# Logit slots of whole keys in two parts instead of three, with a new order

## The chip, the core and the metric

The kernel runs on one core of a Trainium2 chip. The metric is the device time of one execution in microseconds. A core has five engines that work side by side and wait for each other by semaphores: TensorE (PE, with its weight loads as PEld), VectorE (DVE), ScalarE (ACT), GpSimd (POOL) and SyncE (SP, which here only issues transfers).

## What is computed

The input `x` has 2048 tokens of 512. One branch is attention with a compressive memory: 32 heads of 16, four segments of 512 tokens, causal softmax within a segment, and a memory `M`, `z` of all earlier segments. The other is a gated MLP with 1792 hidden columns. A gate per token mixes both.

```python
phi = lambda t: jnp.where(t > 0, t + 1.0, jnp.exp(t))
for s in range(N):
    logits = jnp.einsum('bhqd,bhkd->bhqk', qs, ks) * scale + mask
    p = _softmax(logits, axis=-1)
    a_dot = jnp.einsum('bhqk,bhkd->bhqd', p, vs)
    num = jnp.einsum('bhld,bhde->bhle', phi(qs), M)
    den = jnp.einsum('bhld,bhd->bhl', phi(qs), z)[..., None] + 1e-06
    outs.append(g * num / den + (1.0 - g) * a_dot)
    M = M + jnp.einsum('bhld,bhle->bhde', phi(ks), vs)
    z = z + jnp.einsum('bhld->bhd', phi(ks))
...
h = _gelu(x @ w_gate) * (x @ w_up)
return gate * (o @ wo) + (1 - gate) * (h @ w_down)
```

## The kernel before

**Tasks and their order.** The kernel is a list of some 1340 tasks. The string ORDER (L35 on) names them one by one, and `Sched.run` issues them in that order; each engine works through its own tasks in it and waits where data or a buffer is not ready. A word is a name, then `#` with the letters of the buffers that it takes (in the order of its allocations), and `@A`, `@D`, `@P` or `@S` where a task may run on several engines: ACT, DVE, POOL or SP. The numbers in a name are mostly segment and part: `up2.8` is the product with columns 8 x 128 of `w_up` for segment 2.

**TensorE's tasks.** `q`, `k`, `v`, `gt` and `up` are products of a segment with weights (`gt` two column blocks at once), `dn` and `wo` accumulate one output tile of 128 tokens: 14 `dn` steps and then four `wo` steps, which read the attention output that `o` has written into `xT`. Nearly all run as four matmuls side by side on tiles of 32 columns of the array (`mm4`, L389); I call such four a batch. `den`, `num` and `M` belong to the memory. The last segment's last output tile is split in 384 (`h0`) and 128 columns (`h1`).

**Slots.** Causal logits of a segment are computed in 18 logit slots, nine for each pair of chunks of eight heads. A slot is a PSUM tile of two halves of [128, 2, 512]: `lg` writes it (L695; four heads side by side on tiles of 32 rows, one bank each), `ex...a` and `ex...b` take the exponential of each half on ACT into a `pT` buffer (L231), and `as...a`, `as...b` set what lies above the diagonal to zero on POOL. Keys come in four tiles of 128. For each, the 64 queries beside the first half of the keys are put into a slot of their own (`e == 2`, mask at L722); the rest, 448, 320, 192 and 64 queries for the four key tiles, fills two whole-key slots (`e` 0 for even heads, 1 for odd ones), by the table FULL: each entry is key tile, offset, columns, and place in the slot. Only the first 64 columns of a key tile lie on the diagonal. With three parts a slot, tile 0 was split so that both masked stretches of the slot begin 256 columns apart, and one POOL operation of four stretches of 64 masks a half (L727):

```python
FULL = (((0, 0, 256, 0), (3, 0, 64, 256), (0, 256, 192, 320)),
        ((1, 0, 256, 0), (2, 0, 192, 256), (1, 256, 64, 448)))
```

**From slot to output.** `pv` (L756) multiplies the parts of its slots with the values, for the even (`e`) or odd (`o`) heads of a chunk: six whole-key parts and four of 64 queries, in the order PVO. On DVE, `epv` transposes the result (L773), `r`, `rg` and `n` divide by the sum and weigh (L783, L786, L791), `m` adds the memory part (L796, DVE or POOL), and `o` transposes into `xT` (L799). `pv3.3o` is the last of the 32 groups, and `o3.3` the last `o`. `os` scales an output tile, `st` stores it.

**Buffers.** Slots, `gt` and `num` share three pairs of PSUM banks (`lg`, letters a to c); the other products have two banks (`gen`). `pT` has eleven buffers. `wos` scales a part of `wo` once, `ke` and `ko` make key copies for odd heads, `vh` makes value copies, `ek`, `eq` and `ev` take products out of PSUM.

Of the kernel before, what the change touches and what calls it, by code (L numbers as in the profile page):

```python
# [9 lines left out]
ALU = mybir.AluOpType  # L10
# [3 lines left out]
P = 128  # L14
D = 512
# [13 lines left out]
HB = P // 2  # L29
# [7 lines left out]
k0f1.0 xt0.1 xt1.1 xt2.1 ext0.1 xt3.1 ext1.1 k0f2.0 ext2.1 ext3.1 k0f3.0 k0f0.1 k0f1.1 k0f2.1  # L37
k0f3.1 q0.0#ba ek0.1@A ek0.3@D ek0.2@D q0.1#a eq0.0@D ke0.2@A#a gt0.0#b eq0.1@A ke0.3@D ek0.0@D
Ek0.1#a ke0.0@D#b ke0.1@D ko0.1@A lg0#ac Emk0.1 v0.2#b Qk0.1@D#a ex0a#a v0.1#a ev0.2@D ex0b#b as0a
ko0.3@D gt0.1#a ko0.0@D as0b ev0.1@D ko0.2@P egt0.0#a gt0.6#c phk0.1@P#a egt0.1#b gt0.3#b egt0.6#c  # L40
gt1.6#a egt0.3#d pk0.1#a v0.0#b egt1.6#e v0.3#a ev0.0@D lg1#cb ev0.3@D q0.2#bb ex1b#c vh0.1@D
q0.3#a eq0.2@D ex1a#d lg2#ab eq0.3@D k1.0#bc ex2b#e as1a lx2 as1b q1.0#ac ex2a#f lg3#cb z1.3
gt0.5#a ex3a#g z1.0 eq1.0@D Ek0.0#a z0.2 v1.0#a ex3b#h Qk0.0@D#a z3.3 gt1.0#c tb z0.0 omg#a
gt0.4#b egt0.5#f lx3 Emk0.0 ev1.0@D z3.2 k1.1#a egt0.4#g z3.0 gt0.2#a z2.1 ek1.0@A z2.2 egt1.0#h
ek1.1@D up0.0#b egt0.2#i z1.2 z1.1 lg4#bc up0.10#a z0.3 gt1.3#a z3.1 ex4b#i z2.3 wo vh0.0@D ex4a#j
gt1.4#c z2.0 z0.1 as4a eup0.10 as2a gt1.1#b egt1.3#j eup0.0 egt1.4#k M0.1#a q1.1#b egt1.1#l eM0.1
as2b up1.0#a eq1.1@D lg5#ac eup1.0 up0.11#b ex5a#k phk0.0@D#a as3b pv0.0e#aa eup0.11 pk0.0#b
Eq1.0#a zsp2 lg6#ba epv0.0e up0.7#b ex6b#a zsp0 up0.6#a eup0.7 ex6a#b as4b up1.3#b as6b eup0.6
ex5b#c as3a Emq1.0 as6a lg7#ab eup1.3 pv0.0o#a as5a ex7a#d as5b up0.3#b epv0.0o ex7b#g as7a lg8#ca
zsp1 eup0.3 pv0.1e#ab ex8b#h Qq1.0@D#a up0.5#b epv0.1e ex8a#i as8b lg9#ba as7b eup0.5 up0.4#a  # L50
ex9b#j as8a zsp3 pv0.1o#b eup0.4 ex9a#a lg10#ca ke1.0@D#b phq1.0@P#a up1.2#a epv0.1o g2 ex10b#b
r0.0#a up1.7#b eup1.2 ex10a#c r0.1#b lg11#ba rg0.0 up1.8#a n0.0#a Ek1.0#a as10a eup1.7 gt2.2#c
wos1@D ex11b#k Emk1.0 eb ex11a#d Qk1.0@D#a gt1.2#a phk1.0@D#a eup1.8 as11a pk1.0#a omz gt1.5#b
egt1.2#m egt2.2#n as9a gt2.4#a ke1.1@D egt1.5#o as11b M0.0#b egt2.4#p up0.1#a eM0.0 v1.3#b as9b
eup0.1 as10b lg12#cb ev1.3@D k1.2#aa ex12b#e rg0.1 ko1.1@D zbd0 q1.2#ba ex12a#f ek1.2@D as12b
wos2@P mbd0 lg13#ab eq1.2@A q1.3#a wdn3 ex13b#g pv0.2e#ba as12a eq1.3@D ex13a#h as13b lg14#cb
epv0.2e v1.1#a ex14a#i as13a up0.8#b ev1.1@D ex14b#a lg15#ac eup0.8 up1.13#a ex15b#b as14b as14a
pv0.2o#b ex15a#c eup1.13 lg16#bc epv0.2o up0.12#a ex16b#j n0.1#b up1.9#b ex16a#e r0.2#a as16b
eup0.12 as15b lg17#ac as15a eup1.9 v1.2#a ex17b#f ko1.0@D wos3@D pv0.3e#bb ex17a#g ev1.2@D as17b
lg18#bc as16a epv0.3e up0.13#a ex18a#h as17a ke1.2@D#a ko1.2@D k1.3#b Eq1.1#a eup0.13 wdn0 wos0@D  # L60
# [12 lines left out]
dn0.0.6 dn0.0.7 o0.3 dn0.0.8 ex31b#g up2.6#b Eq2.0#a lg32#bc eup2.6 dn0.0.9 dn0.0.10 as28b
dn0.0.11 ex31a#h dn0.0.12 as30b dn0.0.13 wo0.0.0 as31b pv1.2e#ba ex32a#i as31a wo0.0.1 as30a
wo0.0.2 epv1.2e wo0.0.3 ex32b#a lg33#ab os0.0@D#a up2.5#b ex33a#b ke2.0@D#b st0.0 r1.1#b pv1.2o#a
eup2.5 ex33b#c lg34#ca epv1.2o k2.2#bc ex34a#j ko2.0@D as33b dn0.3.0#a dn0.3.1 ek2.2@D as32b
dn0.3.2 ex34b#e as32a lg35#bc rg1.1 as33a Emq2.0 dn0.3.3 dn0.3.4 ex35a#f dn0.3.5 as34b n1.1#a
M1.1#b dn0.3.6 dn0.3.7 ke2.1@A eM1.1 lg36#ab ke2.2@D#a Qq2.0@D#a dn0.3.8 ex36b#g dn0.3.9
phq2.0@D#c dn0.3.10 dn0.3.11 dn0.3.12 ex36a#h dn0.3.13 pv1.3e#bb wo0.3.0 ex35b#a epv1.3e lg37#ba
as36a wo0.3.1 as35a wo0.3.2 as34a wo0.3.3 ex37b#b k2.3#b rma1.2 os0.3@D#b ex37a#c num1#ca v2.1#a  # L80
enum1.1#b rma1.3 ko2.1@A ek2.3@D gt2.5#b Ek2.0#a as35b enum1.0#a ev2.1@A as37a rmr1 pv1.3o#b
gt3.1#c rmg1 Emk2.0 epv1.3o egt2.5#t nm1.0@D#a ko2.2@A up1.10#a Qk2.0@D#a m1.0@P egt3.1#u
enum1.2#a up2.7#b eup1.10 nm1.1@P#b lg38#bc r1.3#a v2.2#a eup2.7 ex38a#i enum1.3#b dn0.2.0#b
dn0.2.1 dn0.2.2 rg1.3 phk2.0@D#a dn0.2.3 ev2.2@A lg39#ab ex38b#a nm1.2@D#c dn0.2.4 pk2.0#a dn0.2.5
dn0.1.0#a r1.2#b dn0.1.1 dn0.1.2 ke2.3@D ex39b#d zbd1 dn0.1.3 vh2.1@D dn0.1.4 dn0.2.6 rg1.2
dn0.2.7 ex39a#e o1.0 as39b lg40#cb dn0.2.8 as38a dn0.2.9 Ek2.1#a dn0.2.10 dn0.2.11 dn0.2.12
dn0.2.13 wo0.2.0 ex40a#f wo0.2.1 wo0.2.2 dn0.1.5 dn0.1.6 Qk2.1@A#a as38b dn0.1.7 dn0.1.8 dn0.1.9
gt3.5#a vh2.0@A ex40b#j as39a gt3.0#c as36b m1.1@P wo0.2.3 as40a egt3.5#a gt2.0#b os0.2@D#c as37b
as40b n1.3#b egt3.0#b st0.2 o1.1 dn0.1.10 dn0.1.11 egt2.0#i dn0.1.12 pv2.0e#bb dn0.1.13 wo0.1.0
epv2.0e wo0.1.1 wo0.1.2 wo0.1.3 Emk2.1 lg41#ac os0.1@D#a up2.9#b ex41b#k mbd1 st0.1 n1.2#a k3.2#aa  # L90
ex41a#b st0.3 eup2.9 m1.2@P lg42#bc ek3.2@D pv2.0o#b ex42a#c phk2.1@P#a up3.10#a epv2.0o ex42b#g
lg43#ab eup3.10 up2.11#b ex43b#h as41b pk2.1#b M2.0#a ex43a#d as41a lg44#cb eM2.0 as43b eup2.11
up2.0#a as42a ex44a#e as42b q2.3#b nm1.3@P#a eup2.0 ex44b#f r2.0#a lg45#ac as43a eq2.3@D pv2.1e#aa
ex45b#j as44b m1.3@D up2.13#b as44a epv2.1e Eq2.1#a lg46#bc eup2.13 q3.0#aa ex46b#b Emq2.1 ko2.3@D
q3.1#b Qq2.1@D#a eq3.0@A o1.3 phq2.1@P#a ex46a#c pv2.1o#a gt3.2#c epv2.1o ex45a#g eq3.1@A as46b
Eq3.0#a den2#aa lg47#ba eden2 up2.10#b ex47a#k Qq3.0@D#a Emq3.0 up2.3#a phq3.0@D#b ex47b#a as47a
gt3.3#b eup2.10 o1.2 rg2.0 gt3.4#a egt3.3#d as45a eup2.3 as45b egt3.2#g as47b M2.1#b v3.3#a
egt3.4#f eM2.1 k3.0#bb ev3.3@D as46a lg48#bc ek3.0@D rma2.0#a v3.2#a ex48a#d dn1.0.0#b dn1.0.1
ev3.2@D ex48b#e rma2.2 dn1.0.2 lg49#ab r2.1#b k3.1#a rg2.1 ex49a#f ke3.0@D#b n2.1#b dn1.0.3
dn1.0.4 ek3.1@D ex49b#h as49a lg50#ca as48a dn1.0.5 dn1.0.6 as48b ex50a#i pv2.2e#aa as49b dn1.0.7  # L100
rma2.3 dn1.0.8 epv2.2e ex50b#b dn1.0.9 dn1.0.10 lg51#bc up3.7#a ex51a#c rma2.1 dn1.0.11 ex51b#g
dn1.0.12 eup3.7 lg52#ab as50b dn1.0.13 rmr2 wo1.0.0 ex52a#j pv2.2o#a as51b wo1.0.1 wo1.0.2 epv2.2o
ex52b#d as52a wo1.0.3 num2#ca as50a v3.1#a as51a os1.0@A#c enum2.1#b r2.2#b ko3.1@A q3.2#bb
enum2.0#a ev3.1@A lg53#bc eq3.2@D q3.3#a ex53a#e rg2.2 n2.0#a up3.8#b eq3.3@A ke3.1@D rmg2 ex53b#f
nm2.0@P#b pv2.3e#ab eup3.8 gt3.6#b epv2.3e as52b as53a enum2.3#a as53b nm2.1@P#c pv2.3o#b egt3.6#c
up2.1#a epv2.3o m2.1@P lg54#cb eup2.1 up3.13#b ko3.0@P enum2.2#b ex54a#h up3.3#a eup3.13 ex54b#b
r2.3#a lg55#ac eup3.3 k3.3#b ex55b#c as54b up3.11#a as54a ek3.3@D ex55a#g as55b lg56#bc eup3.11
v3.0#b ex56b#i as55a o2.1 up3.0#a m2.0@D ev3.0@A n2.2#b ex56a#a lg57#ac zbd2 eup3.0 up3.6#b
# [88 lines left out]
def kernel(  # L197
# [15 lines left out]
    nc = tc.nc  # L213
# [39 lines left out]
    S = Sched(RINGS)  # L253
# [419 lines left out]
    def logit_slot(s, t):  # L673
# [25 lines left out]
        for i in cs:  # L699
            c = 2 * pr + i  # L700
# [423 lines left out]
```

## Time and profile before

| | us |
|---|---|
| median of 3 runs (266.87 to 267.15) | 267.0 |
| the profiled execution | 266.52 |
| its span, first to last instruction | 264.6 |
| pT, 144 exponentials on ACT, L231 | 137.9 busy |
| L722, 32 masks of the 64-query slots on POOL | 37.5 busy |
| L617, 56 products with G on DVE | 38.3 busy |

Rows of groups give the line, engine and operation, then output and inputs with their shapes, the count, after the bar the time in which at least one ran, the mean of one in ns, and after the second bar the idle time of the engine just before. Rows of a timeline or of the chain of waits begin with the start and the length in us and merge neighbours of one kind. Rows of windows give busy time and, in brackets, the count by engine. Rows of waits give the total in us, how often, and the longest. Matmuls overlap, so the length of one is more than the distance to the next.

### The profile page before, as it was taken

How to read it: one execution, taken by the hardware profiler on the slowest of the kernel's cores; microseconds unless marked ns; L12 is line 12 of the kernel's file. 1: busy time of each engine (PE TensorE's matmuls, PEld its weight loads, DVE VectorE, ACT ScalarE, POOL GpSimd, SP SyncE). 2: the span in 40 equal slices, each digit the busy share in tenths (PEclk: the TensorE clock that was granted, in tenths of full speed). 3: DMA queues.
4: the chain of work that ended last, by engine and by line, in shares of the span. 5: the costliest groups of instructions: out<-in, count | busy, mean ns of one | idle time of the engine just before them, and what ended most of it. 6: DMA issues, size and time to landing. Idle time of an engine off the chain costs nothing.

```text
span 264.6 us, 13767 instructions
## 1 busy us (share of the span) xinstructions
PE 260.2 (98%) x6300; PEld 140.7 (53%) x6300; DVE 176.5 (67%) x360; ACT 218.8 (83%) x255; POOL 148.6 (56%) x266
## 2 busy tenths in 40 slices
PE   8999999999999999999999999999999999999995
PEld 7644575555555555455554455555444555555553
DVE  1634895889479688767695277765878684576461
ACT  2598989999999999999999999999999989840002
POOL 8360106886633762785454746698486768829100
PEclk9999999999999999999999999999999999999999
DMA  7999974300500005200005012000000000001002
GB/s 232 349 210 319 206 85 102 43 7 19 145 5 2 2 5 132 72 5 22 6 2 42 21 46 43 2 5 2 5 4 2 2 5 22 22 26 63 22 22 82
DMA packets 23706, 15.96 MB, mean 60 GB/s; under 512 B 14048, under 2 KB 22624, under 8 KB 23648
## 3 DMA queue, kind: packets, MB, share of 16 engines
q1 hardware_dynamic: 22640, 14.30, 23.8%
q8 instruction: 49, 0.80, 1.3%
q10 hardware_dynamic: 1008, 0.79, 0.9%
q14 instruction: 9, 0.07, 0.1%
HBM read 9.84 MB, written 2.10 MB: 45 GB/s over the span
## 4 chain that ended last, share of the span: by engine, by line
PE 97%; ACT 1%; DVE 1%; issue 0%
PE dn L389 24%; PE up L389 19%; PE gt L389 18%; PE lg L695 9%; PE pv L756 7%; PE v L389 6%; PE q L389 5%; PE k L389 4%; PE k L385 2%; PE warm L385 1%; ACT pT L231 1%; PE q L385 1%; PE gt L385 1%; PE M L874 1%; PE xt L491 0%; PE num L965 0%
## 5 line engine op out<-in xcount | busy, mean ns | idle before, releaser
L231 ACT ACTIVATE pT<-lg 128x1024 bf16<-128x1024 f32 x144 | 137.9, 1026 | 5.8 <-PE lg L695 4.9
L727 POOL TENSOR_SCALAR_AFFINE_SELECT pT<-pT 128x256 bf16<-128x256 bf16 x128 | 53.1, 439 | 63.2 <-ACT pT L231 59.0
L389 PE MATMUL dn<-wdn,G 128*32 128x512 bf16 (+2 forms) x952 | 58.1, 367 | 0.0
L389 PE MATMUL up<-xT,wup 128*32 128x512 bf16 x896 | 57.1, 380 | 0.0
L389 PE MATMUL gt<-xT,wga 128*32 128x512 bf16 x864 | 49.4, 379 | 0.0
L617 DVE TENSOR_TENSOR G<-up,G 128x512 bf16<-128x512 f32 x56 | 38.3, 684 | 14.2 <-PE up L389 13.2
L722 POOL TENSOR_SCALAR_AFFINE_SELECT pT<-pT 64x1024 bf16<-64x1024 bf16 x32 | 37.5, 1173 | 9.6 <-ACT pT L231 8.5
L389 PEld LDWEIGHTS <-wga 128*32 128x32 bf16 x864 | 24.5, 97 | 21.1 <-issue 0.2
L389 PEld LDWEIGHTS <-G 128*32 128x32 bf16 x952 | 22.7, 96 | 20.4 <-issue 0.2
L389 PEld LDWEIGHTS <-wup 128*32 128x32 bf16 x896 | 22.0, 96 | 18.8 <-issue 0.2
L773 DVE STREAM_TRANSPOSE T<-pv 128x512 f32<-128x512 f32 x32 | 22.9, 714 | 12.8 <-PE pv L756 12.6
L231 ACT ACTIVATE G<-gt 128x1024 bf16<-128x1024 f32 x28 | 27.7, 1018 | 3.7 <-PE gt L389 3.5
L1027 ACT ACTIVATE osb<-dn,omz 128x512 bf16<-128x512 f32 (+1 forms) x4 | 2.5, 614 | 25.3 <-PE dn L389 25.3
L229 ACT ACT_TABLE_LOAD x18 | 23.1, 1283 | 0.3
L1029 DVE TENSOR_SCALAR osb<-dn,omz 128x512 bf16<-128x512 f32 (+1 forms) x13 | 9.6, 740 | 17.8 <-PE dn L389 17.8
L756 PE MATMUL pv<-pT,vz 128*32 128x256 bf16 (+2 forms) x768 | 20.8, 238 | 0.0
L756 PEld LDWEIGHTS <-vz 128*32 128x32 bf16 x768 | 16.3, 97 | 6.6 <-ACT qT L235 0.7
L389 PE MATMUL dn<-wo,xT 128*32 128x512 bf16 (+2 forms) x272 | 19.2, 367 | 0.0
L389 PEld LDWEIGHTS <-xT 128*32 128x32 bf16 x528 | 12.8, 96 | 11.2 <-issue 0.5
L695 PEld LDWEIGHTS <-kO 32*128 32x128 bf16 x640 | 9.7, 92 | 15.1 <-issue 14.2
L934 POOL TENSOR_SCALAR rm<-Tm 32x32 f32<-32x32 f32 x48 | 14.1, 294 | 5.1 <-DVE Tm L928 2.0
L695 PE MATMUL lg<-qT,kO 32*128 32x64 bf16 (+2 forms) x640 | 16.4, 217 | 0.1
(112 smaller groups left out, 330.2 us busy)
## 6 DMA issues: line engine op xcount, KB each, us to landing
wup<-in_B_w_up_dram SPq DMA_DIRECT2D x1, 1792.0 KB, 9.8
out_dram<-osb SPq DMA_DIRECT2D x14, 128.0 KB, 1.7
wdn<-in_B_w_down_dram SPq DMA_DIRECT2D x3, 512.0 KB, 5.3
wga<-in_B_w_gate_dram SPq DMA_DIRECT2D x1, 1280.0 KB, 9.6
wdn<-in_A_x_dram SPq DMA_DIRECT2D x2, 512.0 KB, 10.2
wq<-in_A_wq_dram SPq DMA_DIRECT2D x1, 512.0 KB, 5.5
wga<-in_B_w_gate_dram SPq DMA_DIRECT2D x1, 512.0 KB, 6.4
wv<-in_A_wv_dram SPq DMA_DIRECT2D x1, 512.0 KB, 6.7
```

The lines of the kernel that those rows point to most:

```text
L229: nc.scalar.activation(nil[0][:, 1:2], nil[0][:, 0:1], func)
L231: nc.scalar.activation(dst, src, func, **kw)
L385: nc.tensor.matmul(out, lhsT=lhsT, rhs=rhs, start=start, stop=stop)
L389: nc.tensor.matmul(out[a], lhsT=lhsT[:, a], rhs=rhs, start=start, stop=stop, tile_position=(0, 32 * j), skip_group_check=True)
L617: UPT[(s, hs)] = evac("DVE", g, box, lambda e, t: nc.vector.tensor_mul(G[(s, hs // 2)][:, hs % 2, :], t[:, :], G[(s, hs // 2)][:, hs % 2, ...
L695: nc.tensor.matmul(A[j // 2][:, j % 2, at:at + n], lhsT=l, rhs=q[a, i, q0:q0 + n], start=True, stop=True, tile_position=(32 * j, 0))
L722: nc.gpsimd.affine_select(out=v, in_=v, pattern=[[0, 16], [1, HB]], compare_op=ALU.is_ge, fill=0.0, base=0, channel_multiplier=-1)
L727: nc.gpsimd.affine_select(out=v, in_=v, pattern=[[0, 4], [1, HB]], compare_op=ALU.is_ge, fill=0.0, base=HB, channel_multiplier=-1)
L756: nc.tensor.matmul(t[m:m + 32, q0:q0 + n], lhsT=v, rhs=pT[(s, u, j // 2)][:, j % 2, at:at + n], start=(n_ == 0), stop=(n_ == len(parts) - ...
L773: nc.vector.transpose(TT[key][:, e, :, :].rearrange("p a b -> p (a b)"), t[:, :])
L934: eng_of[e].tensor_scalar_add(RMt[s][32 * ((j + c) % 4):32 * ((j + c) % 4) + 32, c, :, :], bx["Td"][32 * c:32 * c + 32, :, 2 * j:2 * j + 2 ...
L1029: nc.vector.tensor_scalar_mul(bx["o"][:, lo:hi], box["t"][:, 0:hi - lo], g)
```

## The change

FULL has two parts a slot: 448 and 64 columns, or 320 and 192. `lg` issues 8 matmuls for a whole-key slot where it issued 12, `pv` 32 where it issued 40. The masked stretches of a slot no longer lie at equal distance, so `fa` issues two POOL operations per half, each of two stretches of 64. `Sched`, the slots, the buffers and all other tasks are the same; ORDER is another order of the same 1342 words, with other buffer letters and engines for some.

```diff
-    PVO = (0, 1, 2, 5, 3, 6, 4, 7, 8, 9)
-    FULL = (((0, 0, 256, 0), (3, 0, 64, 256), (0, 256, 192, 320)),
-            ((1, 0, 256, 0), (2, 0, 192, 256), (1, 256, 64, 448)))
+    PVO = (0, 1, 2, 4, 3, 5, 6, 7)
+    FULL = (((0, 0, 448, 0), (3, 0, 64, 448)), ((1, 0, 320, 0), (2, 0, 192, 320)))
...
-                v = pt[:, :, :].rearrange("p h (g n) -> p (h g) n", g=2)[:, :, 0:HB]
-                nc.gpsimd.affine_select(out=v, in_=v, pattern=[[0, 4], [1, HB]],
-                                        compare_op=ALU.is_ge, fill=0.0, base=HB,
-                                        channel_multiplier=-1)
+                for at in (0, FULL[w][1][3]):
+                    v = pt[:, :, at:at + HB]
+                    nc.gpsimd.affine_select(out=v, in_=v, pattern=[[0, 2], [1, HB]],
+                                            compare_op=ALU.is_ge, fill=0.0, base=HB,
+                                            channel_multiplier=-1)
```

Of ORDER, the stretch from the last pv group on:

```diff
-pv3.3o#a dn3.2.6 dn3.2.7 epv3.3o dn3.2.8 dn3.2.9 dn3.2.10 r3.3#a dn3.2.11 rg3.3 n3.3#a dn3.3h0.12
-dn3.2.12 dn3.3h0.13 dn3.1.9 m3.3@D dn3.0.10 o3.3 dn3.2.13 wo3.2.0 wo3.2.1 dn3.1.10 dn3.1.11
-wo3.3h0.0 wo3.3h0.1 dn3.0.11 wo3.2.2 dn3.0.12 wo3.2.3 dn3.0.13 wo3.0.0 os3.2@D#a wo3.3h0.2 wo3.0.1
+dn3.0.3 wo3.1.1 pv3.3o#a dn3.2.8 dn3.2.9 epv3.3o dn3.2.10 wo3.1.2 dn3.2.11 r3.3#a dn3.2.12 rg3.3
+n3.3#a dn3.0.4 dn3.2.13 wo3.2.0 m3.3@D wo3.2.1 wo3.2.2 o3.3 dn3.0.5 dn3.3h0.11 dn3.3h0.12
+dn3.3h0.13 wo3.2.3 dn3.0.6 dn3.0.7 os3.2@A#b wo3.3h0.0 dn3.0.8 wo3.3h0.1 dn3.0.9 st3.2@S dn3.0.10
```

Engines that change, by kind, before and after: `ek` on ACT 3 and 7 of 16, `eq` on ACT 5 and 2, `ev` on ACT 4 and 5, `ke` on ACT 3 and 4, `ko` on ACT 4 and 5 and on POOL 3 and 5, `vh` on ACT 2 and 0, `wos` on ACT 0 and 2 and on POOL 1 and 2, `os` on ACT 4 and 7, `m` on POOL 6 and 5, the sums of `phi` (`phk`, `phq`) on POOL 5 and 3; the rest of each is on DVE. On ACT after are `ev1.1`, `ke1.3`, `wos1` and `wos3`, which were not, and no longer `eq1.2` and `vh1.0`.

## The prediction

> **What bounds the kernel now.** I read the page's totals and slices first, then its chain of work that ended last, and the waits between engines.
>
> ```profile
> span 264.6 us, 13767 instructions
> PE 260.2 (98%) x6300; PEld 140.7 (53%) x6300; DVE 176.5 (67%) x360; ACT 218.8 (83%) x255; POOL 148.6 (56%) x266
> PE   8999999999999999999999999999999999999995
> ACT  2598989999999999999999999999999989840002
> PEclk9999999999999999999999999999999999999999
> PE 97%; ACT 1%; DVE 1%; issue 0%
> PE dn L389 24%; PE up L389 19%; PE gt L389 18%; PE lg L695 9%; PE pv L756 7%; PE v L389 6%; PE q L389 5%; PE k L389 4%; PE k L385 2%; PE warm L385 1%; ACT pT L231 1%; PE q L385 1%; PE gt L385 1%; PE M L874 1%; PE xt L491 0%; PE num L965 0%
> ```
>
> TensorE is busy in every slice at full granted clock, and the chain of waits runs 97% through it. So the time is the sum of TensorE's stream plus whatever makes it wait; a microsecond saved elsewhere is worth nothing unless TensorE waits for it. It hardly does: once it has started, the longest waits of its side for another engine are these.
>
> ```profile
> PEld L756 <- ACT qT L235: 0.7, 2, 0.3
> PEld L695 <- POOL pT L727: 0.4, 1, 0.4
> ```
>
> Two things can therefore move the time: the length of the stream, and new waits made by the new order. ACT is nearly as full as TensorE up to slice 34, so the order has little room there.
>
> **The shorter stream.** Both FULL slots go from three parts to two, and the parts of pv with them from ten to eight. In the built program TensorE has 512 matmuls fewer (5788 for 6300): 64 whole-key slots lose one batch of four, and 32 pv groups lose two. That is 128 batches; the columns that pass are the same (448+64 and 320+192 are 512, as 256+64+192 were). What is a batch worth beyond its columns?
>
> ```profile
> L389 PE MATMUL up<-xT,wup 128*32 128x512 bf16 x896 | 57.1, 380 | 0.0
> L756 PE MATMUL pv<-pT,vz 128*32 128x64 bf16 x256 | 10.1, 193 | 0.0
> 15.09 6.91 PE gt L389 x128
> ```
>
> The mean of one matmul is 380 ns at 512 columns and 193 at 64, so a column costs 187/448 = 0.417 ns. The chain has 128 gt matmuls, 32 batches of four side by side, in 6.91 us: 216 ns a batch, of which 512 x 0.417 = 213.7 are columns. About 2.2 ns are left for the batch itself. The timeline around a slot and two pv groups says the same for small ones:
>
> ```profile
> 100.35 0.40 PE L695 MATMUL lg<-qT,kT 16*128 16x256 bf16 x12
> 100.68 0.54 PE L756 MATMUL pv<-pT,vz 128*32 128x256 bf16 x20
> 101.05 0.20 PE L756 MATMUL pv<-pT,vh 128*32 128x64 bf16 x4
> 101.08 0.26 PE L756 MATMUL pv<-pT,vz 128*32 128x192 bf16 x4
> 101.16 0.26 PE L756 MATMUL pv<-pT,vh 128*32 128x64 bf16 x12
> 101.25 1.04 PE L389 MATMUL up<-xT,wup 128*32 128x512 bf16 x16
> ...
> 104.10 0.40 PE L695 MATMUL lg<-qT,kO 32*128 32x256 bf16 x12
> 104.43 1.05 PE L389 MATMUL up<-xT,wup 128*32 128x512 bf16 x16
> ```
>
> A batch of 64 columns takes 0.03 us from start to start (101.05 to 101.08), three take 0.09 (101.16 to 101.25), and 64 x 0.417 + 2.2 is 28.9 ns. A slot holds TensorE 0.33 us (104.10 to 104.43), though its columns and three batches are 0.22; the other 0.11 us is the passage between a slot's tiles of 32 rows and the neighbours' tiles of 32 columns. It stays: both orders have 72 slots apart from each other. So the stream shrinks by 128 x 2.2 ns = **0.28 us**. Bounds: nothing, if loading weights for a long batch costs what the batch saved, and 128 x 29 ns = 3.7 us, if a removed batch gave back the whole time of a small one. I take 0.28, which the 64- and the 512-column rows both give.
>
> The page "TensorEngine Tiling (Array Packing)" of the Trainium skill, section "Instruction Overhead", gives each matmul an overhead of about 60 cycles. By that, and the 2.4 GHz of its page "TensorE: Matmul & The Clock Gate", the removed batches would be worth about 128 x 25 ns = 3.2 us as an estimate, and the time would be near 263.8. The trace disagrees: the 2 ns above.
>
> **The masks.** Each whole-key mask becomes two GpSimd operations of 128 columns.
>
> ```profile
> L727 POOL TENSOR_SCALAR_AFFINE_SELECT pT<-pT 128x256 bf16<-128x256 bf16 x128 | 53.1, 439 | 63.2 <-ACT pT L231 59.0
> L340 POOL TENSOR_SCALAR_AFFINE_SELECT wdn<-wdn 128x128 bf16<-128x128 bf16 x1 | 0.3, 294 | 0.1
> 41.60:60.00 18.40, 5.04 (x13) 1.00 0.24 48
> core 0: us, PE busy (x) PEld busy (x) DVE busy (x) ACT busy (x) POOL busy (x), PEclk, DMA share, GB/s
> 41.60:60.00 18.40, 18.40 (x536) 10.29 (x532) 13.13 (x25) 18.32 (x24) 15.75 (x34) 1.00 0.24 48
> 60.00:85.00 25.00, 25.00 (x644) 13.51 (x640) 19.02 (x43) 23.80 (x27) 13.19 (x21) 1.00 0.18 45
> 85.00:113.00 28.00, 27.90 (x706) 14.45 (x708) 21.67 (x40) 27.18 (x31) 16.35 (x31) 1.00 0.19 50
> ```
>
> The one select of 128x128 took 294 ns, so a pair is 588 where one mask took 439: +149 ns, 128 times, 19 us more on POOL. Bounds: no more than the 439 of now, and twice 439 = 878 if the price is all per operation. I take 588, from the row of the same size. The cover is POOL's idle time. It is thinnest from 41.6 to 60 us (the first window row of the fence is L727 alone): 15.75 of 18.40 us busy, 2.65 idle, 13 masks. At 588 they add 1.9 us and fit; TensorE sees nothing but masks that end 0.15 us later. The cover is gone at 439 + 2650/13 = 643 ns a pair. Behind a late mask stand, on POOL, the next masks and the memory sums, and pv on TensorE waits for them.
>
> The page "SBUF — State Buffer" of the Trainium skill, section "Who interferes with whom", says that VectorE and GpSimd hold a shared port pair exclusively, the loser waiting for the whole instruction. It speaks against the change, which asks for the pair twice as often; by it the excess of the 439 over an undisturbed select would come twice per mask.
>
> **The order.** Work changes engines. Up to the last slot ACT gets four k evacuations, one v evacuation, two kO copies and two wo scalings more, and three q evacuations and two vh copies less. POOL gets two kO copies and a wo scaling more and three large additions less, DVE loses most. The places on ACT that matter:
>
> ```profile
> L235 ACT ACTIVATE vz<-v 128x512 bf16<-128x512 f32 x4 | 2.5, 614 | 0.0
> L235 ACT ACTIVATE qT<-q 128x512 bf16<-128x512 f32 x5 | 3.0, 597 | 0.0
> L241 ACT ACTIVATE kO<-kT,odd 128x512 bf16<-128x512 bf16 x4 | 2.9, 732 | 0.0
> L235 ACT ACTIVATE vh<-vz 64x1024 bf16<-64x1024 bf16 x2 | 2.1, 1056 | 0.0
> ```
>
> Between 60 and 113 us ACT gains wos1 and wos3 (priced by the kO row of the same size, 0.73 each), ev1.1 (0.61) and ke1.3 (under 0.73), and loses eq1.2 (0.60) and vh1.0 (1.06): +1.1 us at most. Its idle time there is 1.20 + 0.82 = 2.0 us. It fits, with 0.9 left, so I cost it at nothing; without that cover the exps come late, and with them the banks for the next slots. Bounds: -0.4 us, if the small waits on these rows go, to +1.1.
>
> The tail does not fit. Every output's last product needs o3.3, the end of a chain on DVE after the last pv group.
>
> ```profile
> 252.39 0.53 PE L756 MATMUL pv<-pT,vz 128*32 128x256 bf16 x20
> 252.95 2.66 PE L389 MATMUL dn<-wdn,G 128*32 128x512 bf16 x48
> ...
> 253.20 0.72 DVE L773 STREAM_TRANSPOSE T<-pv 128x512 f32<-128x512 f32 x1 [0.61 <-PE pv L756]
> 253.95 0.35 DVE L783 RECIPROCAL r<-T 128x32 f32<-128x32 f32 x1
> 254.34 0.19 DVE L786 TENSOR_TENSOR r<-r,G 128x32 f32<-128x32 f32 x1
> 254.57 0.69 DVE L791 TENSOR_TENSOR N<-T,r 128x512 bf16<-128x512 f32 x1
> 255.29 0.42 DVE L796 TENSOR_TENSOR N<-N,Nm 128x512 bf16<-128x512 bf16 x1
> 255.75 0.71 DVE L799 STREAM_TRANSPOSE xT<-N 128x512 bf16<-128x512 bf16 x1
> ```
>
> From the first matmul behind pv3.3o (252.95) to the end of o3.3 (255.75 + 0.71) are 3.51 us. Before, 17 batches of 512 columns and 4 of 384 stand between pv3.3o and wo3.2.3, the first that reads o3.3: 17 x 0.216 + 4 x 0.162 = 4.32 us, 0.8 to spare. After, the order has 12 and 3 there: dn3.2.8 to dn3.2.13, wo3.1.2, dn3.0.4, dn3.0.5, wo3.2.0 to wo3.2.2, and dn3.3h0.11 to 13: 2.59 + 0.49 = 3.08 us. The same six steps stand on DVE in both. TensorE so waits **0.43 us** at wo3.2.3, and all outputs of the last segment are queued behind it. Bounds: nothing, if pv3.3o's chain finds DVE quicker, and 0.6 with a weight load that has to follow the wait.
>
> **Sum.** -0.28 + 0.43 + 0 (masks) + 0 (ACT) = +0.15 us. The profiled execution took 266.52 us (span 264.6 and 1.9 around it), so 266.67; it lies 0.48 under the median of the runs, so for the median 267.0 + 0.15, **267.2 us**. No change means here within 0.2%, 266.47 to 267.53; this is what a measurement of this kernel can tell.
>
> **Rivals.**
> *Masks late (slower).* If a pair costs more than 643 ns, POOL falls behind from 41.6 to 60 us and pv waits. At 730, halfway to the bound, 13 x 0.29 - 2.65 = 1.1 us, so 268.3; at 878 3.1 us, 270.2. For it: selects already take 439 in the mean, far from 294 for 128 columns. Against: half of that is columns.
> *ACT late (slower).* wos1 or wos3 ahead of an exp delays it by 0.73 us where ACT is 97% full: 267.9. Against: the 0.9 us left.
> *Fewer waits (faster).* The new order drops the two waits of TensorE's side above (0.7 and 0.4) or the tail finds its work in time: -0.28 - 0.4, 266.3. Against: the tail sum.
> *A batch has a large price of its own (faster).* 3.7 us, 263.3; that is the bound above, and the rule of the tiling page is its reading. The 64-column rows are against it.
> *The stream doesn't shrink.* Then 267.0 + 0.43 = 267.4.
>
> **How the numbers follow.** Forecast 0.45 (of it 0.34 within 0.2%, 0.09 slower, 0.02 faster, for small waits of some 0.4 us either way; its own range 266.7 to 267.7); masks 0.20; ACT 0.12; fewer waits 0.18 (0.15 faster, 0.03 same); large batch price 0.02; no shrinking 0.03 (0.02 same, 0.01 slower). Faster 0.02 + 0.15 + 0.02 = 0.19, same 0.34 + 0.03 + 0.02 = 0.39, slower 0.09 + 0.20 + 0.12 + 0.01 = 0.42. The range reaches from the fewer-waits case to the lower half of the masks' case: 266.4 to 269.0.
>
> **What would show it.** TensorE with 5788 matmuls; a slot still near 0.33 us and a pv group a few ns shorter; L727's successor 256 times near 300 ns, POOL near 168 us busy; a wait of about 0.4 us for DVE's transposition into xT, some 5 us before the last matmul. I am wrong if pv or lg waits for POOL or ACT by more than half a microsecond, if that wait is absent, or if a slot loses tens of ns.

## The result, and the profile after

The changed kernel took 267.87 us (median of 8 runs, 267.41 to 269.01) beside 266.80 of the kernel before on the same chip (8 runs, 266.40 to 267.15): a ratio of 1.0047, 95% interval 1.0033 to 1.0061. That is 0.9 to 1.6 us slower, outside the 0.2% that count as no change. The forecast was 267.2, with 266.4 to 269.0 as its range and 0.42 for slower. The profiled execution took 267.68 us, 1.16 more than the one before.

The page of the changed kernel, in its lines of totals, chain and groups:

```profile
span 265.8 us, 12883 instructions
PE 260.2 (98%) x5788; PEld 128.6 (48%) x5788; DVE 175.4 (66%) x353; ACT 222.1 (84%) x262; POOL 164.9 (62%) x394
PE 88%; POOL 4%; DMA 3%; DVE 1%; ACT 1%; issue 1%; DVEq 0%; POOLq 0%
L727 POOL TENSOR_SCALAR_AFFINE_SELECT pT<-pT 128x128 bf16<-128x128 bf16 x256 | 69.6, 308 | 63.0 <-ACT pT L231 61.9
L389 PE MATMUL dn<-wo,xT 128*32 128x512 bf16 (+2 forms) x272 | 20.1, 367 | 0.4 <-DVE xT L799 0.4
```

TensorE has its 512 matmuls fewer and is as long busy as before, in part because a matmul that waits for its data counts as busy here (the row of 1.09 us below). The chain says more: 97% of it ran through TensorE, now 88%, and POOL and transfers, which had no part in it, have 7% together.

To separate the start from the rest I take two rows of TensorE's timeline in every profile: the first batch of `v` (the start) and the last four batches of `wo` with 128 columns (the end of the work). Behind the latter come 3.6 us in both kernels. A bracket at the end of a row gives the idle time of the engine ahead of it, and what ended that. Before:

```profile
13.18 1.91 PE L389 MATMUL v<-wv,xT 128*32 128x512 bf16 x32
260.97 0.40 PE L389 MATMUL dn<-wo,xT 128*32 128x128 bf16 x16
```

and after, with the two places between them at which TensorE lost the most, a `pv` group at 180.7 us and the tail:

```profile
13.67 1.91 PE L389 MATMUL v<-wv,xT 128*32 128x512 bf16 x32
...
180.68 1.09 PE L756 MATMUL pv<-pT,vz 128*32 128x448 bf16 x12
181.58 0.22 PE L756 MATMUL pv<-pT,vh 128*32 128x64 bf16 x4
181.61 0.27 PE L756 MATMUL pv<-pT,vz 128*32 128x192 bf16 x4
181.69 0.28 PE L756 MATMUL pv<-pT,vh 128*32 128x64 bf16 x12
181.78 1.05 PE L389 MATMUL dn<-wdn,G 128*32 128x512 bf16 x16
...
254.05 0.82 PE L389 MATMUL dn<-wdn,G 128*32 128x512 bf16 x12
...
256.42 0.88 PE L389 MATMUL dn<-wdn,G 128*32 128x512 bf16 x16
257.69 0.40 PE L389 MATMUL dn<-wo,xT 128*32 128x512 bf16 x4 [0.39 <-DVE xT L799]
...
262.15 0.40 PE L389 MATMUL dn<-wo,xT 128*32 128x128 bf16 x16
```

The start is 0.49 us later, and from there to the end it takes 248.48 us instead of 247.79, 0.69 more. The `pv` group (pv2.2e) holds TensorE from 180.68 to 181.78, 1.10 us, where a group takes 0.57 elsewhere (100.94 to 101.51 in the same profile): 0.53 lost. At the tail one batch of 512 columns and three of 384 begin at 256.42 (one row, since neighbours are merged). They are 0.216 + 3 x 0.162 = 0.70 us, and the next begins at 257.69 instead of 257.12: 0.57 lost, 0.56 by the single matmuls. With -0.28 for the shorter stream that makes +0.81; the 0.12 to 0.69 would be small waits of the old order that are gone, which I did not trace one by one.

What was late for pv2.2e, POOL's timeline ahead of it:

```profile
172.43 2.34 POOL L721 TENSOR_SCALAR_AFFINE_SELECT pT<-pT 64x1024 bf16<-64x1024 bf16 x2
174.85 1.78 POOL L934 TENSOR_SCALAR rm<-Tm 32x32 f32<-32x32 f32 x4
176.71 2.35 POOL L721 TENSOR_SCALAR_AFFINE_SELECT pT<-pT 64x1024 bf16<-64x1024 bf16 x2
179.14 1.63 POOL L934 TENSOR_SCALAR rm<-Tm 32x32 f32<-32x32 f32 x4
180.84 1.03 POOL L727 TENSOR_SCALAR_AFFINE_SELECT pT<-pT 128x128 bf16<-128x128 bf16 x4
```

POOL never stops here, and the pair that pv2.2e needs (as45b) comes behind four steps of the memory (rma2.1, the row at 179.14). Two of the group's 32 matmuls began at once; the next waited until 181.18 for the first operation of the pair, and the ones behind them until 181.43 for the second.

### The profile page after: what moved, and what is told of

Same layout as the page of the kernel before. It is cut to its first block, busy times and chain, and to the rows that moved or that the text cites. A ratio compares the mean times of both kernels' runs of the same rounds, so it can differ in the third digit from the quotient of the medians.

```text
span 265.8 us, 12883 instructions
## 1 busy us (share of the span) xinstructions
PE 260.2 (98%) x5788; PEld 128.6 (48%) x5788; DVE 175.4 (66%) x353; ACT 222.1 (84%) x262; POOL 164.9 (62%) x394
## 4 chain that ended last, share of the span: by engine, by line
PE 88%; POOL 4%; DMA 3%; DVE 1%; ACT 1%; issue 1%; DVEq 0%; POOLq 0%
PE dn L389 23%; PE up L389 18%; PE gt L389 16%; PE lg L694 8%; PE pv L756 7%; PE v L389 5%; PE q L389 5%; PE k L389 3%; DMA wq<-in_A_wq_dram 2%; POOL pT L721 2%; POOL rm L934 2%; DMA wdn<-in_A_x_dram 1%; PE q L385 1%; PE gt L385 1%; ACT pT L231 1%
## 5 line engine op out<-in xcount | busy, mean ns | idle before, releaser
L727 POOL TENSOR_SCALAR_AFFINE_SELECT pT<-pT 128x128 bf16<-128x128 bf16 x256 | 69.6, 308 | 63.0 <-ACT pT L231 61.9
L389 PEld LDWEIGHTS <-wga 128*32 128x32 bf16 x864 | 23.3, 97 | 21.7 <-issue 0.4
L1027 ACT ACTIVATE osb<-dn,omz 128x512 bf16<-128x512 f32 (+2 forms) x7 | 4.3, 628 | 24.0 <-PE dn L389 24.0
L756 PE MATMUL pv<-pT,vz 128*32 128x320 bf16 (+3 forms) x512 | 21.0, 274 | 0.1
L389 PE MATMUL dn<-wo,xT 128*32 128x512 bf16 (+2 forms) x272 | 20.1, 367 | 0.4 <-DVE xT L799 0.4
L934 POOL TENSOR_SCALAR rm<-Tm 32x32 f32<-32x32 f32 x48 | 15.3, 318 | 5.3 <-DVE Tm L928 2.2
L756 PEld LDWEIGHTS <-vz 128*32 128x32 bf16 x512 | 12.5, 97 | 11.2 <-issue 2.3
L1029 DVE TENSOR_SCALAR osb<-dn,omz 128x512 bf16<-128x512 f32 x10 | 7.5, 747 | 15.4 <-PE dn L389 14.1
L389 PE MATMUL v<-wv,xT 128*32 128x512 bf16 x256 | 16.4, 380 | 0.0
L694 PE MATMUL lg<-qT,kO 32*128 32x64 bf16 (+3 forms) x512 | 16.3, 231 | 0.1
```

Source lines behind the costliest of these rows:

```text
L389: nc.tensor.matmul(out[a], lhsT=lhsT[:, a], rhs=rhs, start=start, stop=stop, tile_position=(0, 32 * j), skip_group_check=True)
L694: nc.tensor.matmul(A[j // 2][:, j % 2, at:at + n], lhsT=l, rhs=q[a, i, q0:q0 + n], start=True, stop=True, tile_position=(32 * j, 0))
L727: nc.gpsimd.affine_select(out=v, in_=v, pattern=[[0, 2], [1, HB]], compare_op=ALU.is_ge, fill=0.0, base=HB, channel_multiplier=-1)
L756: nc.tensor.matmul(t[m:m + 32, q0:q0 + n], lhsT=v, rhs=pT[(s, u, j // 2)][:, j % 2, at:at + n], start=(n_ == 0), stop=(n_ == len(parts) - ...
L934: eng_of[e].tensor_scalar_add(RMt[s][32 * ((j + c) % 4):32 * ((j + c) % 4) + 32, c, :, :], bx["Td"][32 * c:32 * c + 32, :, 2 * j:2 * j + 2 ...
L1029: nc.vector.tensor_scalar_mul(bx["o"][:, lo:hi], box["t"][:, 0:hi - lo], g)
```

## The experiments

Each kernel had 12 runs (e11 6, the changed kernel 8) beside runs of the kernel before on the same chip; the ratio is to those, with its 95% interval. It is not the quotient of the medians, from which it can differ by 0.2% (those of e1 are 267.59 and 266.95). "First v" and "from there" are the two rows above, from one profile each.

| kernel | ratio | first v, us | from there, us |
|---|---|---|---|
| before | 1 | 13.18 | 247.79 |
| before again (e12) | 1.0012 (0.9990 to 1.0033) | 13.50 | 247.72 |
| changed | 1.0047 (1.0033 to 1.0061) | 13.67 | 248.48 |
| changed again (e11) | 1.0045 (1.0028 to 1.0061) | 13.06 | 248.45 |
| e1, new parts and pairs, old order | 1.0005 (0.9983 to 1.0028) | 13.43 | 248.63 |
| e2, old parts, new order | 1.0044 (1.0025 to 1.0062) | 13.65 | 249.12 |
| e3, changed, tail moved | 1.0029 (1.0007 to 1.0051) | 13.77 | 249.67 |
| e4, changed, one mask operation | 1.0032 (1.0008 to 1.0055) | 13.42 | 248.27 |
| e5, before with pairs | 1.0003 (0.9985 to 1.0020) | 13.36 | 247.96 |
| e6, new parts alone | 0.9974 (0.9960 to 0.9988) | 13.55 | 247.43 |
| e7, changed, both moves | 1.0006 (0.9985 to 1.0028) | 14.18 | 247.51 |
| e8, e1 with m1.3 on POOL | 0.9999 (0.9986 to 1.0013) | 13.56 | 247.88 |
| e9, e8 with rma2.1 on DVE | 0.9992 (0.9974 to 1.0009) | 13.26 | 247.66 |
| e10, e7 with the old opening | 1.0006 (0.9991 to 1.0021) | 13.96 | 248.84 |

The last column agrees to 0.07 us between the two profiles of the kernel before and to 0.03 between those of the changed one, and so can tell apart what the runs' scatter of 0.2% does not. But one profile can hold a wait that others of the same order lack: e2, e3 and e4 each lost 0.2 us near 20.4 us, and later ones are named where they come. So I go by the places at which TensorE loses time, not by the sum alone.

**The halves of the change.** e1 is the changed kernel with the order of before, e2 the kernel before with the new order:

```diff
 # e1, against the changed kernel
-ORDER = """ (the new order)
+ORDER = """ (the order of before)
 # e2, against the kernel before
-ORDER = """ (the order of before)
+ORDER = """ (the new order)
```

> The parts and mask pairs of the change, with the order of the kernel before. Theory A (four separate items: a shorter stream -0.28 us, a wait for o3.3 in the new order +0.56, a wait of pv2.2e for masks +0.53, the rest in the first 15 us): no wait for o3.3; mask pairs in an order that was not made for them, pv waiting for masks at one or two places, 0 to 0.8 us in all; so -0.3 to +0.5 us against the kernel before. Rival B (the parts with their masks cost it all, whatever the order): +1.0 us or more. Rival C (the order costs it all): -0.3 us.

> The order of the change, with three parts a slot and one mask operation per half as before. Theory A: the wait for o3.3 is there (0.4 to 0.6 us), none at pv2.2e: +0.4 to +0.7 us against the kernel before. Rival B: no difference. Rival C: +1.2 us or more.

e2 costs what the whole change costs (1.0044, 1.2 us), as rival C expected and more than theory A's 0.4 to 0.7. It has the tail's wait of 0.56 us, so the tail belongs to the order alone. Theory A expected no wait at pv2.2e, but there is one of 0.27, shown with e4 below. Another 0.55 us at 78.6 us, in no other profile, stayed unexplained. e1 has no wait at the tail and is not to be told from before in time. Its profile however shows two waits that neither kernel has. From the slot ahead of `q` at 163.65 to `q` at 164.92 it takes 1.27 us, where before has 0.33, so 0.94 are lost; from `num` to `v` at 187.31 it takes 0.60 instead of 0.37, so 0.23 are lost. (The expectations say 1.04 and 0.36, which counts time that both steps take in the kernel before too.) Together that is 1.17 of the 1.20 us by which its last column lies above that of e6, the same kernel with one mask operation. e5, e8 and e9 are about these waits.

**The tail and the mask, one at a time.** e3 lets three `dn` steps pass ahead of wo3.2.3, e4 puts the single mask operation back, which leaves the second part of a slot unmasked:

```diff
 # e3
-dn3.3h0.13 wo3.2.3 dn3.0.6 dn3.0.7 os3.2@A#b wo3.3h0.0 dn3.0.8 wo3.3h0.1
+dn3.3h0.13 dn3.0.6 dn3.0.7 dn3.0.8 wo3.2.3 os3.2@A#b wo3.3h0.0 wo3.3h0.1
 # e4
-                for at in (0, FULL[w][1][3]):
-                    v = pt[:, :, at:at + HB]
-                    nc.gpsimd.affine_select(out=v, in_=v, pattern=[[0, 2], [1, HB]],
+                v = pt[:, :, :].rearrange("p h (g n) -> p (h g) n", g=2)[:, :, 0:HB]
+                nc.gpsimd.affine_select(out=v, in_=v, pattern=[[0, 4], [1, HB]],
```

> The changed kernel with three batches (dn3.0.6, dn3.0.7, dn3.0.8) moved ahead of wo3.2.3, the first to read o3.3. Theory A: the wait of 0.56 us at wo3.2.3 is gone and nothing takes its place: 0.4 to 0.56 us faster than the changed kernel, so +0.5 to +0.9 us against the kernel before. Rival: the wait moves to another of the last outputs and the end is the same, +1.2 us.

> The changed kernel with one mask operation per half at columns 0 and 256, as before the change; the second part of each slot stays unmasked and 64 columns of the first are set to zero in places, which changes the output and no other instruction. POOL's price for the masks is that of before. Theory A: pv2.2e does not wait for masks any more: 0.4 to 0.6 us faster than the changed kernel. Rival C (order alone): the same time as the changed kernel, +1.2 us against before.

In e3 the tail's wait is gone and pv2.2e waits as before it (0.54 us). But its profile took 249.67 us, because of another wait, on DVE and then on TensorE:

```profile
242.06 0.81 SPq L998 DMA_DIRECT2D out_dram<-osb  x2
246.18 0.75 DVE L1029 TENSOR_SCALAR osb<-dn,omz 128x512 bf16<-128x512 f32 x1 [3.41 <-DMA out_dram<-osb]
246.98 0.54 PE L756 MATMUL pv<-pT,vz 128*32 128x448 bf16 x12 [1.37 <-DVE osb L1029]
```

An output tile is scaled on DVE into a buffer that a store must have left; the store, begun at 242.06, landed 4.0 us later, and `pv` behind it needed the bank that this scaling empties: 1.54 us lost. (It also lost the 0.2 us near 20.4.) In the changed kernel the same scaling waits too, only shorter, and in the kernel before the one at this place waits for its own product and for no store:

```profile
243.64 0.75 DVE L1029 TENSOR_SCALAR osb<-dn,omz 128x512 bf16<-128x512 f32 x1 [1.15 <-DMA out_dram<-osb]
```
```profile
244.78 0.75 DVE L1029 TENSOR_SCALAR osb<-dn,omz 128x512 bf16<-128x512 f32 x1 [1.32 <-PE dn L389]
```

All seven profiles of the new order have this wait for a store on DVE. In five it is 1.1 to 1.2 us and costs nothing; in e3 and e10 it is 3.4 and 3.2 us and costs TensorE 1.54 and 1.31. None of the seven profiles of the old order has it.

What goes with a late store can be read in the traces. The row above is of two stores, issued 0.44 us apart, and each lands in 16 parts. In e3 15 parts of the first had landed by 243.79 and the last at 246.05, and in between, from 243.22 on, a transfer of 16 KB in the queue that the profile calls `instruction` (q8) took 1.65 us. Such a transfer comes in every profile of this order. It begins 1.0 and 1.2 us after the first store's issue in e10 and e3, where the first store is late; 1.3 to 1.7 us after it in the changed kernel, e11, e4 and e7, where the first lands in 1.7 us and the second, for which no engine waits, in 3.4 to 3.6; and 2.0 us after it in e2, where neither is late. So the lateness goes with the moment of that transfer. That the transfer is its cause is not shown, for no run moved it.

In e4 the tail's wait stands (0.56). At pv2.2e I compare the time from the group's first matmul to the slot behind it, with the same tasks between them in all profiles of this order. The changed kernel, e4, e2, and e7 (below), which has no wait there:

```profile
180.68 1.09 PE L756 MATMUL pv<-pT,vz 128*32 128x448 bf16 x12
182.77 0.40 PE L694 MATMUL lg<-qT,kT 16*128 16x320 bf16 x8
```
```profile
180.57 0.65 PE L755 MATMUL pv<-pT,vz 128*32 128x448 bf16 x8
182.38 0.40 PE L694 MATMUL lg<-qT,kT 16*128 16x320 bf16 x8
```
```profile
181.55 0.81 PE L756 MATMUL pv<-pT,vz 128*32 128x256 bf16 x20
183.35 0.40 PE L695 MATMUL lg<-qT,kT 16*128 16x256 bf16 x12
```
```profile
181.16 0.53 PE L756 MATMUL pv<-pT,vz 128*32 128x448 bf16 x12
182.69 0.40 PE L694 MATMUL lg<-qT,kT 16*128 16x320 bf16 x8
```

These are 2.09, 1.81, 1.80 and 1.53 us. So theory A is wrong here too: with one mask operation about 0.27 us of the wait are left, with new parts and with old. The order, which sets as45b behind rma2.1, makes half of the wait by itself, and the pairs add the other half, 0.28 us. That is as much as the shorter stream gains, which fits that e2 and the whole change cost the same.

**The parts, the pairs, and both moves.** e5 is the kernel before with two mask operations (columns 0 and 256), e6 is e1 with one, again with the second part unmasked, e7 the changed kernel with e3's edit and a second one:

```diff
 # e5
-                v = pt[:, :, :].rearrange("p h (g n) -> p (h g) n", g=2)[:, :, 0:HB]
-                nc.gpsimd.affine_select(out=v, in_=v, pattern=[[0, 4], [1, HB]],
+                for at in (0, 4 * HB):
+                    v = pt[:, :, at:at + HB]
+                    nc.gpsimd.affine_select(out=v, in_=v, pattern=[[0, 2], [1, HB]],
 # e7, beside e3's
-ev3.2@D ex48a#f dn1.0.2 lg49#ab rma2.1 n2.1#b k3.1#a ex49a#g dn1.0.3 dn1.0.4 ek3.1@D as45b ex49b#h
+ev3.2@D ex48a#f dn1.0.2 lg49#ab as45b rma2.1 n2.1#b k3.1#a ex49a#g dn1.0.3 dn1.0.4 ek3.1@D ex49b#h
```

> The kernel before with its parts and its order, and only the mask of each whole-key half as two POOL operations of two stretches instead of one of four. In the profile of the new parts in the old order TensorE lost 1.04 us at 163.8 us (q behind the DVE transpose that frees its bank; the DVE product N at L796 before it took 1.72 us instead of 0.40, from 0.09 us into a run of six mask operations that start without a break until 0.27 us behind the last of them) and 0.36 us at 186.7 us (v behind the reciprocal of rm, whose POOL steps came 1.0 us later). Theory A, the pairs alone make both: two operations of one mask leave DVE no break, and POOL's queue at 171 to 186 us grows by 0.15 us a mask. It expects L727 at 256 times about 300 ns, POOL near 165 us busy, both waits at the same places (0.8 to 1.1 us and 0.2 to 0.5 us), and a time 0.8 to 1.4 us over the kernel before. Rival B, the shorter TensorE stream runs ahead of its partners and meets them early: no such waits here, time within 0.3 us of before. Rival C, these waits are chance of one execution: none or others, time as before.

> The new parts in the order of before with the single mask operation of before, so that the second part of each whole-key slot stays unmasked and the output differs. Theory A: only the stream shrinks. No wait at q near 163 us and none at v near 186 us, N at L796 about 0.42 us long there, POOL near 148 us busy, and a time 0.1 to 0.4 us under before (128 batches of 2.2 ns are 0.28 us). Rival B: the waits of 1.04 and 0.36 us are there as with the pairs, time 0.5 to 1.2 us over before. If a batch were worth 25 ns (60 cycles of 0.417 ns), 3.2 us under before.

> The changed kernel with two moves in its order: three dn steps ahead of wo3.2.3, so that o3.3 has 0.65 us more, and the mask task as45b ahead of the POOL task rma2.1 (1.6 us of steps). Theory A, the two waits are what the new order costs: neither the wait of 0.56 us at wo3.2.3 nor that of 0.53 us in pv2.2e, no wait over 0.2 us in their place, and a time 0.9 to 1.2 us under the changed kernel, so within 0.3 us of the kernel before. Rival C, the 1.2 us are start-up and scatter: waits gone and time still 0.6 us or more over before. Rival D, the mask moved forward only moves the wait to rm: a wait at num or den behind rm2, 0.3 us or more.

e6 is the shorter stream by itself: 0.36 us less from the first `v` on (0.29 less than in the second profile of before), neither of e1's waits, and the one ratio whose interval lies below 1. e7 has neither wait left, with nothing above 0.09 us in their place (184.98 us), and needs 247.51 us: 0.97 less than the changed kernel, and 0.28 less than before. Rival D is out, and so is C as far as the work behind the start goes. Its ratio, 1.0006, does not show the 0.28: the interval is wide, and its profile started the latest of all; how its other runs started is not known.

e5 is a miss for theory A. The wait at `v` is there (0.20 us lost ahead of 186.49), so the pairs alone make it; the wait at `q` is not. Rival C holds for that one. What e1 and e5 show there are two outcomes of one meeting. In e1, DVE and POOL:

```profile
162.52 1.72 DVE L796 TENSOR_TENSOR N<-N,Nm 128x512 bf16<-128x512 bf16 x1
```
```profile
162.43 1.53 POOL L727 TENSOR_SCALAR_AFFINE_SELECT pT<-pT 128x128 bf16<-128x128 bf16 x6
```

and in e5:

```profile
162.61 0.47 DVE L797 TENSOR_TENSOR N<-N,Nm 128x512 bf16<-128x512 bf16 x1
```
```profile
162.51 1.70 POOL L728 TENSOR_SCALAR_AFFINE_SELECT pT<-pT 128x128 bf16<-128x128 bf16 x6
```

The product N begins 0.1 us into a run of six mask operations both times. In e1 it ends at 164.24, only after the run's end at 163.96; in e5 it comes through behind the first, and the run is 0.17 us longer instead. The transposition behind N frees the bank that `q` needs, so e1 lost 0.94 us. In before and in e6 the same product met a run of three single masks and took 0.42. Which of the two happens with pairs is not settled.

**A version of the old order.** e8 and e9 give the two tasks that meet POOL to another engine:

```diff
 # e8, against e1
-m1.3@D
+m1.3@P
 # e9, against e8
-rma2.1
+rma2.1@D
```

> The new parts with mask pairs in the order of before, with one task on another engine: m1.3 (the product N at L796 that took 1.72 us on DVE) on POOL, where it takes 1.16 us. Theory A: DVE goes straight on to the transpose, q does not wait at 163 us, the 0.36 us at 187 us stays; TensorE's other waits as in before; 1.0 us under the new parts in the old order by the profile, so about 0.1 us over before less 0.28 us of stream: within 0.4 us of before. Rival: POOL, 1.16 us later, gives masks late to pv2.1o (near 167 us), a wait of 0.3 us or more there, and the time stays where it was.

> The new parts with mask pairs in the order of before, m1.3 on POOL as in the run ahead, and rma2.1 (four of the steps behind rm2) on DVE, which stood idle for 1.5 us there. POOL's last four steps are then over 1.3 us earlier. Theory A (the pairs cost the old order only where POOL's queue is too late, here the reciprocal of rm, 0.64 us idle DVE and 0.35 us of TensorE at v, 186.1 us): the wait at v goes, nothing takes its place over 0.1 us, first v batch to last batch 0.25 to 0.40 us shorter than before's 247.79, ratio 0.997 to 1.000. Rival: DVE's four steps push G or epv2.2o behind, a wait of 0.2 us or more at 182 to 187 us, time as with the run ahead or over it.

In e8 the wait at `q` is gone and the one at `v` stands (0.22 us lost). It comes from a reciprocal on DVE that waits for POOL's last steps of rm; in e9 DVE does four of them itself while idle, and the wait is gone. e8, then e9:

```profile
185.12 0.95 DVE L939 RECIPROCAL rm<-rm 128x128 f32<-128x128 f32 x1 [0.64 <-POOL rm L934]
```
```profile
182.05 0.74 DVE L934 TENSOR_SCALAR rm<-Tm 32x32 f32<-32x32 f32 x4
183.50 0.69 DVE L617 TENSOR_TENSOR G<-up,G 128x512 bf16<-128x512 f32 x1 [0.71 <-PE up L389]
184.10 0.94 DVE L939 RECIPROCAL rm<-rm 128x128 f32<-128x128 f32 x1
```

e9 is the fastest complete kernel of the study, 266.31 us beside 266.81, but its interval holds 1, and from the first `v` it is 0.13 us shorter than before, not the 0.25 to 0.40 expected. One move made a new wait, in e8 too: with m1.3 on POOL, two masks come later, at 164.37 in e9. The step of DVE on `E` beside them (L829) took 0.98 us where before has 0.42, `pq` on POOL ended only at 168.00, and `den`, which reads it, took 0.52 us (167.86 to 168.38) where before has 0.33: 0.19 lost.

**The start, and both kernels again.** e10 is e7 with the opening of before:

```diff
-k0f1.0 xt0.1 xt1.1 xt2.1 ext0.1 xt3.1 k0f2.0 ext3.1 ext2.1 k0f3.0 ext1.1 k0f0.1
+k0f1.0 xt0.1 xt1.1 xt2.1 ext0.1 xt3.1 ext1.1 k0f2.0 ext2.1 ext3.1 k0f3.0 k0f0.1
```

> The changed kernel with both moves (wo3.2.3 later, as45b earlier), and the words of the opening in before's order: ext1.1 ahead of k0f2.0, ext2.1 ahead of ext3.1. From the first v batch on it should take 247.5 us as the run with both moves did, 0.28 less than before. Open is the start: first v batch at 13.2 to 13.6 us in five profiles of the old order and 13.4 to 14.2 in five of the new. If the words of the opening make that, its first v batch comes at 13.2 to 13.6 and its time is 0.3 us under the run with both moves (ratio 0.997 to 1.000); if it is the landing of the first transfers, which no order decides, it falls anywhere in 13.2 to 14.2 and the ratio is 0.998 to 1.003.

> The changed kernel once more, for a second profile. If its waits are set by the order: 0.5 us in pv2.2e at 180.7 us and 0.56 us at wo3.2.3 again, first v batch to last batch 248.3 to 248.7 us. If they are chance: other waits, and other lengths. The first v batch at 13.4 to 14.2 us if the start scatters by landings, 13.6 to 13.8 if the order sets it. Ratio 1.003 to 1.006.

> The kernel before once more, for a second profile: first v batch to last batch 247.7 to 247.9 us, no wait over 0.3 us behind the first 15 us. The first v batch at 13.2 us again if the order sets the start, 13.2 to 14.2 us, likeliest 13.5, if the landing of the first transfers does. Ratio 0.999 to 1.001.

The changed kernel has its waits a second time, 0.53 us in pv2.2e and 0.56 at wo3.2.3: the order sets them. Its start, though, is the earliest of all 14 profiles (13.06), and the old opening gave 13.96: by these profiles the words of the opening do not make the start. In e7 and e10, the latest two, `q` waits for its weights,

```profile
10.08 1.90 PE L385 MATMUL q<-xT,wq 128*128 128x512 bf16 x7 [0.48 <-DMA wq<-in_A_wq_dram]
```

as here in e10 (0.36 us in e7). But this is not what makes them late: the changed kernel has such a wait too (0.25), and so has e11, the earliest (0.36). No profile of the old order has one. The seven starts of the old order have a mean of 13.41, those of the new of 13.67; with a spread of 1.1 us in the new one this difference is open. e10 also missed its 247.5 us by the late store, 1.31 us; without it, 247.53.

## Why the prediction was right or wrong

The time of 267.87 us lies in the range, and the forecast of 267.2 was 0.67 short of it. Against the kernel before, +0.15 us was forecast and about +1.07 measured; the median that the forecast started from, 267.0 of 3 runs, came out as 266.80 with 8. That the range held is in part luck: it reached up to 269.0 because of late masks at a place where none were late, while the sum itself had the masks at nothing.

*TensorE sets the end: right.* Every difference of the last column that I followed is a wait of TensorE or its stream.

*The shorter stream, -0.28: right.* e6, with everything else taken away, measures -0.29 and -0.36 against the two profiles of before, and 0.3 to 1.1 us by its runs, which allow more than 0.28; the estimate of 3.2 us is out. That e7 gives -0.28 to the digit is partly chance, since its order differs in small waits.

*The masks at 588 ns a pair: nearly right.* They took 2 x 308 = 616, and POOL has 164.9 us instead of the 168 forecast. *Hidden by POOL's idle time: wrong.* The step that failed is "The cover is POOL's idle time. It is thinnest from 41.6 to 60 us". There the masks did hide. The changed kernel, and the second stretch in the kernel before (the fifth pair of each row is POOL):

```profile
41.60:60.00 18.40, 18.40 (x480) 9.22 (x472) 12.53 (x22) 18.33 (x23) 16.70 (x45) 1.00 0.40 61
...
171.20:182.00 10.80, 10.65 (x245) 4.89 (x236) 6.62 (x12) 10.28 (x13) 9.83 (x21) 1.00 0.01 2
```
```profile
171.20:182.00 10.80, 10.80 (x272) 5.42 (x264) 7.16 (x14) 10.76 (x13) 9.73 (x22) 1.00 0.01 3
```

TensorE is busy throughout the first stretch though POOL has 1.7 us idle in 18.4. It waits in the second, which I had not looked at by itself. The reading was wrong from the start: in the kernel before POOL is idle for 1.07 of 10.80 us there, 10%, but for 14% from 41.6 to 60. I had seen it only within 142 to 194 us, where POOL is busy for 70%. What counts besides is how long POOL has worked without a pause when the mask that is needed next comes up, and what the order sets ahead of it. So the masks, which my sum had at 0, cost 0.28 us in pv2.2e, and the order cost 0.27 more there, which was not in the sum either. The rival "masks late" came true in its mechanism, at another place and smaller than its 1.1 to 3.1 us; my condition for it, 643 ns a pair, was not met. By the test that the prediction ends on, a `pv` that waits for POOL by more than half a microsecond, it was wrong here.

*ACT for nothing: right.* TensorE's side waits for ACT in two places, 0.7 us together, as before. *The tail, 0.43: right in mechanism, 0.13 too small.* DVE's chain in the changed kernel:

```profile
254.30 0.72 DVE L773 STREAM_TRANSPOSE T<-pv 128x512 f32<-128x512 f32 x1 [1.48 <-PE pv L756]
...
255.66 0.69 DVE L791 TENSOR_TENSOR N<-T,r 128x512 bf16<-128x512 f32 x1
256.46 0.42 DVE L796 TENSOR_TENSOR N<-N,Nm 128x512 bf16<-128x512 bf16 x1
256.92 0.71 DVE L799 STREAM_TRANSPOSE xT<-N 128x512 bf16<-128x512 bf16 x1
```

From the first matmul behind pv3.3o (254.05) to the end of o3.3 (257.63) it took 3.58 us, not 3.51, since the sum at 256.46 began 0.11 us behind the product ahead of it; and TensorE started 0.06 after the end. Less the 3.08 of batches, which were right, this is 0.56.

*What was not in the sum.* The wait for a store, which the new order brought, and the start. The measured difference is 0.9 to 1.6 us and the profiles show 0.7 behind the start. If the store is late in two executions of seven, as in the profiles, it costs 2/7 of 1.43 = 0.4 us in the mean, an estimate that would close the gap; no run took that wait away, so its share in the measured time is argued, not shown.

So the shorter stream gains 0.3 us, and about 1.1 us of waits are paid for it: 0.56 at the tail and 0.27 in pv2.2e by the order, and 0.28 there by the pairs. Two moves in the order take these back in the profile of e7. That a complete kernel with the new parts is faster than before is not shown: the intervals of e7, e8, e9 and e10 all hold 1.

## What to carry to other kernels

Where one engine is full, a change that takes little from its stream is decided by the places where it must wait, and the idle share of a helper over a long stretch does not find them (POOL was 70% busy from 142 to 194 us, and 90% where the wait came): cut the stretches short, and follow the helper's queue from its last pause to the operation that is needed next. Count the work in an order between the end of each chain and its first reader, and between each store and the next use of its buffer, and leave a margin for the transfers whose landing varies. When the runs scatter as much as the effect, compare stretches of the profile between two fixed points, and find where they part: here two pairs of profiles repeated to 0.07 us, where 12 runs gave 0.2%, but waits of 0.2 to 1.5 us came in single profiles too.

## What the runs showed of the hardware

A DVE operation can be held by a run of POOL operations, not just by one: the product of two arrays in SBUF took 1.72 us, where the kernel before has 0.42, against six masks of 0.30 us that each began some 50 ns before the one ahead had ended. "SBUF — State Buffer" of the Trainium skill, section "Who interferes with whom", has the lock and says that a DVE instruction with two inputs in SBUF contends with a GpSimd instruction that reads it, and that the one that issues first blocks the other for the whole instruction. The trace agrees, but the whole instruction is not the bound: in e1 it was six of them, in e5 one.

The landing of one and the same store of 128 KB took 1.73 us in the changed kernel (issued at 241.79) and 3.99 in e3 (242.06 to 246.05), with the same order up to there. In e3 one of its 16 parts came 2.3 us behind the others, beside a transfer of 16 KB of instructions that began 1.16 us after the store's issue; in the changed kernel that transfer began 1.66 us after it, and the store behind was late instead, 3.38 us. In the kernel before, too, a store issued at 231.05 landed 3.21 us later beside such a transfer (232.10), and nothing waited for it.
